# High parts of q and k stored once and loaded by two transfers, and chains of four pieces between the matrices

## The chip, the cores and the metric

The kernel runs on one core of a Trainium2 chip. The metric is the device time of one execution in microseconds; before the change its median is 2924.13 over three runs (2922.39 to 2925.51). All of the work is on five engines of that core (TensorE or PE, VectorE or DVE, ScalarE or ACT, GpSimd or POOL, and SyncE or SP, which only issues transfers here) and its 16 DMA engines.

## The reference

Two independent results stand side by side in one output of 2048 x 2048: multi-head attention with 32 heads of 32 columns, and a two-dimensional Fourier transform as matrix products.

```python
def _A_ref(x, wqkv, wo):                       # x: 2048 x 1024
    qkv = (x @ wqkv).reshape(B, S, 3, H, Dh) ...
    scores = jnp.einsum("bhqd,bhkd->bhqk", q, k) * scale
    p = _softmax(scores, axis=-1)
    o = jnp.einsum("bhqk,bhkd->bhqd", p, v)
    return o.transpose(...).reshape(B, S, D) @ wo

def _B_ref(x, dft_seq_re, dft_seq_im, dft_hid_re, dft_hid_im):
    a = jnp.einsum("bsd,ed->bse", x, dft_hid_re)
    b = jnp.einsum("bsd,ed->bse", x, dft_hid_im)
    return jnp.einsum("ts,bse->bte", dft_seq_re, a) - jnp.einsum("ts,bse->bte", dft_seq_im, b)
```

All inputs are float32.

## The kernel before

**Arithmetic.** The matrix products take operands rounded to fewer bits, so each operand is split into a high part (the rounded value) and a low part (the rest), and a product is made of three matmuls: high x high, low x high, high x low. The large products (q, k, v, the Fourier matrices, the output projection) are cut by a scheme with seven products in place of eight; its operands are sums and differences of blocks, called pieces here. A piece is loaded (`fetch`), added or subtracted on POOL or DVE, and split by `halves`: the high part by a cast (L501 on DVE, L499 on ACT), the low part by a subtraction (L504). `piece` makes stationary operands in the tile hl, `moving` makes moving operands in a slot (20 numbered buffers, taken through `take_slot`).

**Attention.** For a head h the scores are made twice. `scores(h)` makes them with rows as queries (L1853, tile psS: 32 steps of two matmuls, each followed by a maximum on DVE, L1859, and an exponential on ACT, L1862), which gives each row's maximum and sum. `transposed(h)` makes them again transposed (L1975, psT: 64 matmuls, each with an exponential, L1979) and multiplies the result with v (L1994). The high and low parts of q and k are stacked along the contraction: QS[h % 2] holds q in 96 rows (for each of the 32 components the high, the low and again the high part), KS[h % 2] holds k (high, high, low). So one matmul makes all three products. Rows 96 and 97 of QS take the maxima: zeros (z_d, L2016) for `scores`, then the negative maxima in two parts, which travel over DRAM (store m_d<-lt, L1900; load qs<-m_d, L1901) and open `transposed(h)`. The first four query blocks of `scores(h)` read a copy of the first 512 columns, QX, so that they can begin while QS still serves the head before last.

**q and k over DRAM.** The projections write q and k for four heads at a time: `store_qk(b, j, part, t)` stores a block of 128 rows x 512 columns to `qk_d[b][j]`, a tile [128, 3, 512]. The high part goes out twice in one transfer (L294, a broadcast source, 512 KB), the low part once (L292, 256 KB), so that the three rows of one component lie together. `load_qk` (L312) reads 32 components x 3 = 96 rows of 512 columns in one transfer of 192 KB, eight a head, as soon as the buffers of the head before last are free: one for each quarter of k, after every fourth round of `transposed`, and four for q at its end. `load_x` (L1839) loads QX in the same way.

**The order.** Nothing is ordered on the chip. When the kernel is built, the class `Plan` simulates all engines with costs per operation and emits the instructions of each in the order of this simulation. PE takes from four streams: the score matmuls (S), the transposed ones (T), the value products (V) and the fills, which are all other matmuls (L414). The other engines have heaps: the operations that are ready, lowest rank first, then the earlier ready time. A `Ring` passed as `order` makes the next operation wait until the one before it has begun (`o.soon`); its ready time is then that moment. On the chip each engine runs its list in order, so an instruction that waits holds the ones behind it.

**Around the change.** The Fourier part runs through `dense1`, first with seven outer products of the real matrix, then `between` (two of the second stage's products, p = 1 and 7, eight groups of 24 matmuls each, tile xk_d), then seven of the imaginary matrix. The imaginary half needs the same stationary pieces as the real half, so these are kept in DRAM (ha_d) and loaded again by `again` (L1585). Those that the real half doesn't make by itself are made aside: `aside_c` (L1262) makes chains of four (p = 5, 6, 3, 7; each sum starts from the one before, in three buffers of the tile c) and `aside` (L1303) makes single ones in a slot: two loads, a sum (L1332), for some a store of the sum (si_d, L1338), a cast (L1342), a difference (L1344), and a store of both parts (512 KB). `aside` also makes sums of the Fourier matrix ahead of time ("b" entries), which `load_r` later loads in place of two blocks and a sum. `between` calls `aside` three times in each of 12 groups, for 32 pieces.

## Time and profile before

| | |
|---|---|
| median of three runs | 2924.13 us |
| profiled execution | 2929.45 us, span 2927.7 us |
| granted TensorE clock | 0.999 of full speed |
| DMA traffic | 765.04 MB on the main queue, 79.4% of 16 engines' time |
| read from and written to HBM | 511.74 and 253.25 MB |

Two rows on DMA and one on the largest work of DVE help to place what follows:

```profile
q1 hardware_dynamic: 485452, 765.04, 79.4%
```

```profile
L1859 DVE TENSOR_REDUCE negm<-psS 128x1 f32<-128x1024 f32 x1024 | 1240.7, 1221 | 198.3 <-PE psS L1853 190.1
```

The second is a group of the page: line, engine, operation, tiles and shapes, count, then busy time in us and the mean of one in ns, then the time that the engine stood idle before such instructions and what ended it. A row of the issue list gives tiles, queue, operation, count and KB of one transfer. In the timeline the first number is the start in us from the span's start, the second how long it took. SP's rows are issues: the time to issue a transfer, not to carry it.

### The profile page before, as it was taken

How to read it: one execution, taken by the hardware profiler on the slowest of the kernel's cores; microseconds unless marked ns; L12 is line 12 of the kernel's file. 1: busy time of each engine (PE TensorE's matmuls, PEld its weight loads, DVE VectorE, ACT ScalarE, POOL GpSimd, SP SyncE). 2: the span in 40 equal slices, each digit the busy share in tenths (PEclk: the TensorE clock that was granted, in tenths of full speed). 3: DMA queues.
4: the chain of work that ended last, by engine and by line, in shares of the span. 5: the costliest groups of instructions: out<-in, count | busy, mean ns of one | idle time of the engine just before them, and what ended most of it. 6: DMA issues, size and time to landing. Idle time of an engine off the chain costs nothing.

```text
span 2927.7 us, 47039 instructions
## 1 busy us (share of the span) xinstructions
PE 2904.0 (99%) x14728; PEld 2107.2 (72%) x14728; DVE 2386.5 (82%) x3251; ACT 2373.3 (81%) x4509; POOL 1241.3 (42%) x975
## 2 busy tenths in 40 slices
PE   9999999999999999999999999999999999999999
PEld 8887776777667777777676677667667777777777
DVE  7679888788788887788888898888988788788745
ACT  5348898888888888988999898898889888888741
POOL 2325534142233433337655456666675352243200
PEclk9999999999999999999999999999999999999999
DMA  9989978697789988867899776887876665677558
GB/s 345 349 298 328 314 225 272 222 346 269 268 289 339 309 297 287 291 213 218 291 348 333 226 223 216 276 272 229 271 229 208 204 180 181 193 246 226 188 191 287
DMA packets 485844, 768.18 MB, mean 262 GB/s; under 512 B 120382, under 2 KB 153406, under 8 KB 485470
## 3 DMA queue, kind: packets, MB, share of 16 engines
q1 hardware_dynamic: 485452, 765.04, 79.4%
q8 instruction: 119, 1.95, 0.3%
q14 instruction: 129, 1.06, 0.1%
q10 hardware_dynamic: 144, 0.13, 0.0%
HBM read 511.74 MB, written 253.25 MB: 261 GB/s over the span
## 4 chain that ended last, share of the span: by engine, by line
PE 75%; DMA 4%; DVE 1%; ACT 1%; SPq 0%; issue 0%; POOL 0%; DVEq 0%; ACTq 0%; POOLq 0%
PE pd L414 34%; PE psT L1975 14%; PE pd L1994 13%; PE psS L1853 13%; PE psT L414 2%; ACT psS L1862 1%; DVE negm L1859 1%; DMA qs<-m_d 1%; DMA slot<-in_ct 0%; DMA g<-in_ct 0%; DMA hl<-ha_d 0%; ACT pt L1979 0%; DMA m_d<-lt 0%; DMA ha_d<-slot 0%; DMA g<-g_d 0%
## 5 line engine op out<-in xcount | busy, mean ns | idle before, releaser
L414 PE MATMUL pd<-slot,hl 128*128 128x512 f32 x5028 | 1446.7, 390 | 4.2 <-DMA hl<-ha_d 1.4
L1979 ACT ACTIVATE pt<-psT 128x512 f32<-128x512 f32 x2048 | 1191.5, 668 | 260.7 <-PE psT L1975 258.5
L1859 DVE TENSOR_REDUCE negm<-psS 128x1 f32<-128x1024 f32 x1024 | 1240.7, 1221 | 198.3 <-PE psS L1853 190.1
L1862 ACT ACTIVATE psS<-psS,negm 128x1024 f32<-128x1024 f32 x1024 | 1189.2, 1161 | 47.4 <-DVE negm L1859 44.5
L414 PEld LDWEIGHTS pd<-slot,hl 128*128 128x128 f32 x5028 | 943.6, 188 | 204.8 <-DVE negm L1859 2.7
L1975 PE MATMUL psT<-qs,ks 128*128 128x512 f32 x2048 | 802.4, 395 | 4.4 <-DMA qs<-m_d 3.2
L1975 PEld LDWEIGHTS psT<-qs,ks 128*128 128x128 f32 x2048 | 382.2, 188 | 160.0 <-issue 53.0
L1853 PE MATMUL psS<-ks,qs 128*128 128x512 f32 x1552 | 473.1, 391 | 4.2 <-ACT psS L1862 4.2
L1994 PE MATMUL pd<-pt,vt 128*32 128x512 f32 x4096 | 460.9, 596 | 1.2 <-DVE e L723 0.9
L1853 PEld LDWEIGHTS psS<-ks,qs 128*128 128x128 f32 x1552 | 289.5, 188 | 69.1 <-ACT psS L1862 11.0
L504 POOL TENSOR_TENSOR slot<-raw,slot 128x512 fp32r<-128x512 f32 x153 | 196.2, 1291 | 316.1 <-DVE slot L501 116.6
L1994 PEld LDWEIGHTS pd<-pt,vt 128*32 128x32 f32 x4096 | 123.4, 110 | 285.1 <-issue 268.3
L504 POOL TENSOR_TENSOR slot<-slot,slot 128x512 fp32r<-128x512 f32 x183 | 234.3, 1292 | 206.1 <-DVE slot L501 54.5
L1862 ACT ACTIVATION_READ_ACCUMULATOR psS<-psS,negm 128x1 f32 x1024 | 287.0, 280 | 0.0
L504 POOL TENSOR_TENSOR hl<-raw,hl 128x512 fp32r<-128x512 f32 x122 | 156.8, 1289 | 257.4 <-DVE hl L501 84.7
L479 POOL TENSOR_TENSOR raw<-raw,g 128x512 f32<-128x512 f32 x119 | 153.3, 1291 | 226.6 <-ACT pt L1979 31.3
L414 PE MATMUL pd<-slot,slot 128*128 128x512 f32 x780 | 210.6, 389 | 0.1
L414 PEld LDWEIGHTS pd<-slot,slot 128*128 128x128 f32 x780 | 146.4, 188 | 30.9 <-DVE e L723 0.4
L1853 PE MATMUL psS<-ks,qx 128*128 128x512 f32 x496 | 151.0, 394 | 3.3 <-ACT psS L1862 3.2
L479 DVE TENSOR_TENSOR raw<-raw,g 128x512 f32<-128x512 f32 x141 | 103.3, 738 | 23.6 <-DMA g<-in_ct 6.6
L1853 PEld LDWEIGHTS psS<-ks,qx 128*128 128x128 f32 x496 | 91.7, 188 | 34.6 <-issue 9.2
L479 POOL TENSOR_TENSOR slot<-slot,slot 128x512 f32<-128x512 f32 x79 | 102.1, 1302 | 27.5 <-DVE slot L479 11.3
(140 smaller groups left out, 2167.6 us busy)
## 6 DMA issues: line engine op xcount, KB each, us to landing
hl<-ha_d SPq DMA_DIRECT2D x134, 512.0 KB
slot<-in_ct SPq DMA_DIRECT2D x144, 256.0 KB
qk_d<-e SPq DMA_DIRECT2D x52, 512.0 KB
qs<-qk_d SPq DMA_DIRECT2D x128, 192.0 KB
ks<-qk_d SPq DMA_DIRECT2D x128, 192.0 KB
raw<-g_d SPq DMA_DIRECT2D x96, 256.0 KB
ha_d<-hl SPq DMA_DIRECT2D x42, 512.0 KB
raw<-in_ct SPq DMA_DIRECT2D x80, 256.0 KB
```

The lines of the kernel that those rows point to most:

```text
L414: nc.tensor.matmul(box["ps"], a[1]((a[0].hi, a[0].lo)[u]()), b[1]((b[0].hi, b[0].lo)[v]()), start=k == 0, stop=k == n - 1)
L479: (nc.gpsimd if e == "POOL" else nc.vector).tensor_tensor(out=dest(), in0=dest() if a is None else a.get(), in1=other["q"] if "q" in other ...
L504: (nc.gpsimd if e == "POOL" else nc.vector).tensor_tensor(out=lo(), in0=raw(), in1=f(hi()), op=ALU.subtract)
L1853: nc.tensor.matmul(p[:, i * NB : i * NB + NB], (QX[0] if own else QS[h % 2])[:, qt * P : qt * P + P], KS[h % 2][:, c * 1024 + i * NB : c * ...
L1859: nc.vector.tensor_reduce(out=ST["negm"][:, c, qt : qt + 1], in_=box["p"], axis=AX.X, op=ALU.max, negate=True)
L1862: nc.scalar.activation(box["p"], box["p"], AF.Exp, bias=ST["negm"][:, c, qt : qt + 1], accum_out=ST["sums"][:, c, qt : qt + 1])
L1975: nc.tensor.matmul(box["p"], KS[h % 2][:, t * P : t * P + P], QS[h % 2][:, j * NB : j * NB + NB], start=True, stop=True)
L1979: nc.scalar.activation(box["t"], box["p"], AF.Exp)
L1994: nc.tensor.matmul(po["p"][j * DH : j * DH + DH, :], VT[h][:, k, :], box["t"], start=(k == t0), stop=(k == t), tile_position=(0, j * DH),)
```

## The change

`qk_d` becomes two tiles per block of four heads, [128, 2, 2, 512]: component, part, half, column. Each part is stored once, 256 KB. `rows` puts the 96 rows together by two transfers, now with the 32 components of a part side by side: rows 0 to 63 from both parts in turn (q, x) or from the high part twice (k), and rows 64 to 95 from the part that is left. From head 2 on one pair of transfers covers two quarters (1024 columns: 256 and 128 KB), so a head has four pairs; heads 0 and 1 have eight pairs of half the size. For QX there are two transfers, 128 and 64 KB. The last pair for k is issued at the end of `transposed`, with both pairs for q. A pair is linked by a Ring, so the second waits until the first has begun.

In `between` the 32 single pieces are replaced by eight chains of four, in three sets of two slots each; each of the 12 groups advances each set by one step. `aside_c` takes the chain, the list and the slots as arguments for this. The sums si_d of these pieces are no longer stored and loaded, and a kept piece is stored by two transfers of 256 KB. Six sums of the Fourier matrix are made there too, and the projections make ten more of them ahead (steps 5 and 6 as well).

```diff
-    qk_d = [[dram.tile([P, 3, NB], F32, name=f"qk_d{b}_{j}") for j in range(4)] for b in range(16)]
+    qk_d = [[dram.tile([P, 2, 2, NB], F32, name=f"qk_d{b}_{j}") for j in range(2)] for b in range(16)]
...
-        d = qk_d[b][j]
-        if part:
-            nc.sync.dma_start(d[:, 2 if b % 2 else 1, :], f(t))
+        nc.sync.dma_start(qk_d[b][j // 2][:, part, j % 2], f(t))
+
+    def rows(dst, src, which, again):
+
+        if again:
+            nc.sync.dma_start(dst[2 * DH : 3 * DH], src[:, which])
+        elif which:
+            nc.sync.dma_start(dst[0 : 2 * DH], src[:, 0].rearrange("d (o c) -> o d c", o=1).broadcast_to([2, DH, src.shape[2]]))
         else:
-            nc.sync.dma_start(d[:, 0:2, :] if b % 2 else d[:, 0:3:2, :], f(t).rearrange("p (o n) -> p o n", o=1).broadcast_to([P, 2, NB]))
+            nc.sync.dma_start(dst[0 : 2 * DH], src.rearrange("d i c -> i d c"))
...
-        nc.sync.dma_start(dst[0 : 3 * DH, j * NB : j * NB + NB], qk_d[2 * g + which][j][r0 * DH : r0 * DH + DH].rearrange("d i c -> (d i) c"))
+        src = qk_d[2 * g + which][j // 2][r0 * DH : r0 * DH + DH]
+        rows(dst[:, j * NB : (j + n) * NB], src.rearrange("d i j c -> d i (j c)") if n == 2 else src[:, :, j % 2], which, again)
...
                 if n:
                     aside_c()
-                elif x > 6:
+                else:
                     aside((12, 13, 14))
...
-    def aside_c():
+    def aside_c(chain=chain, todo=todo_c, places=None):
...
-        left = [(pp, p, i, None) for pp in ORDER for p in (5, 6, 3, 7) for i in range(2) if (pp, p, i) not in kept_a]
-        rest = [t for t in todo_a if t[1] == "b"][:0]
...
+        sets = [({}, [], (19, 18)), ({}, [], (17, 16)), ({}, [], (15, 14))]
+        left = [(pp, i) for pp in ORDER for i in range(2) if (pp, 5, i) not in kept_a]
+        for n, (pp, i) in enumerate(left):
+            sets[n % 3][1].extend((pp, p, i) for p in (5, 6, 3, 7))
+        todo_a[:] = [t for t in todo_a if t[1] == "b"][:6]
...
-                    for _ in range(count):
-                        aside((19, 18, 17, 16, 15, 14))
+                    for one in sets:
+                        aside_c(*one)
+                    aside((13, 12))
...
-        got[h, which, j] = op("SP", ISSUE, lambda: load_qk(h, which, j), [*qk_st[2 * g + which][j], *after], [], -2, 192)
+        n = 2 if h > 1 and True else 1
+        both = Ring(1)
+        for again in range(2):
+            o = op("SP", ISSUE, lambda again=again: load_qk(h, which, j, again, n), [*(o for k in range(n) for o in qk_st[2 * g + which][j + k]), *after], [], -2, n * (128 - 64 * again), both)
+        for k in range(n):
+            got[h, which, j + k] = o
...
-                nc.sync.dma_start(f(QX[0])[0 : 3 * DH], qk_d[2 * g][0][r0 * DH : r0 * DH + DH].rearrange("d i c -> (d i) c"))
...
+                rows(f(QX[0]), qk_d[2 * g][0][r0 * DH : r0 * DH + DH, :, 0], 0, again)
...
-            if t % 4 == 3 and h + 2 < H:
-                load_qk_op(h + 2, 1, t // 4, [Tops[h][-1], Sops[h][-1]])
+            if t % 8 == 7 and h + 2 < H:
+                load_qk_op(h + 2, 1, t // 8 * 2, [Tops[h][-1], Sops[h][-1]])
         if h + 2 < H:
-            for j in range(4):
+            for j in (0, 2):
                 load_qk_op(h + 2, 0, j, [Tops[h][-1], Sops[h][-1]])
```

More of the change, by code (lines that the diff above doesn't have):

```diff
@@ L304, with load_qk @@
     nc.gpsimd.memset(rec, 1.0)
-    def load_qk(h, which, j):
+    def load_qk(h, which, j, again, n=1):
         g, r0 = divmod(h, 4)
@@ L1260, with get @@
     chain = {}
-    def aside_c():
-        if not todo_c:
+    def aside_c(chain=chain, todo=todo_c, places=None):
+        if not todo:
             return
-        pp, p, i = todo_c.pop(0)
+        pp, p, i = todo.pop(0)
         rank = seq() + LATER
-        if p == 5:
+        ring = CR if p == 5 and places is None else None
+        if p == 5 and places:
+            chain["n"] = []
+            for k in places:
+                old, users = take_slot(k)
+                box = {}
+                def get(half, k=k, box=box):
+                    if "t" not in box:
+                        box["t"] = slot(k, [P, 2, NB])
+                    return f(box["t"])[:, half]
+                chain["n"] += [[lambda half=half, get=get: get(half), users, old] for half in range(2)]
+            chain["n"] = [chain["n"][2], *chain["n"][:2]]
+        elif p == 5:
             chain["n"] = []
@@ L1291, in aside_c @@
         high = op("DVE", CAST, lambda e: nc.scalar.activation(t().bitcast(F32R), s(), AF.Copy) if e == "ACT" else nc.vector.tensor_copy(t().bitcast(F32R), s()), [made], [us, ut], 10 + rank, other=("ACT", ACAST, 25 + rank), two=True)
-        low = op("POOL", SUB, lambda e: (nc.gpsimd if e == "POOL" else nc.vector).tensor_tensor(out=l().bitcast(F32R), in0=s(), in1=t(), op=ALU.subtract), [high, *wl], [us, ut, ul], rank, 0, CR if p == 5 else None, other=("DVE", ADD, 25 + rank), two=True)
+        low = op("POOL", SUB, lambda e: (nc.gpsimd if e == "POOL" else nc.vector).tensor_tensor(out=l().bitcast(F32R), in0=s(), in1=t(), op=ALU.subtract), [high, *wl], [us, ut, ul], rank, 0, ring, other=("DVE", ADD, 25 + rank), two=True)
         kept_a[pp, p, i] = [op("SP", ISSUE, lambda n=n, r=r: nc.sync.dma_start(ha_d[pp][p][i][:, n * NB : n * NB + NB], r()), [m], [u], rank, 256) for n, (r, m, u) in enumerate(((t, high, ut), (l, low, ul)))]
```

13 lines of the change are left out of this document (6 added, 7 removed).

## The prediction

> **What bounds the kernel now.** I read the page's busy shares and chain first, then what PE loses to waiting, then the DMA share by stage, and last the queue of transfers where one head ends and the next begins.
>
> ```profile
> span 2927.7 us, 47039 instructions
> PE 2904.0 (99%) x14728; PEld 2107.2 (72%) x14728; DVE 2386.5 (82%) x3251; ACT 2373.3 (81%) x4509; POOL 1241.3 (42%) x975
> PE 75%; DMA 4%; DVE 1%; ACT 1%; SPq 0%; issue 0%; POOL 0%; DVEq 0%; ACTq 0%; POOLq 0%
> DMA packets 485844, 768.18 MB, mean 262 GB/s; under 512 B 120382, under 2 KB 153406, under 8 KB 485470
> ```
>
> ```profile
> L414 PE MATMUL pd<-slot,hl 128*128 128x512 f32 x5028 | 1446.7, 390 | 4.2 <-DMA hl<-ha_d 1.4 <-DVE negm L1859 1.3 <-POOL hl L504 0.8
> L1994 PE MATMUL pd<-pt,vt 128*32 128x512 f32 x4096 | 460.9, 596 | 1.2 <-DVE e L723 0.9 <-DVE c L671 0.2
> ```
>
> ```profile
> 2841.29 10.88 PE psT L414 x48
> ```
>
> ```profile
> 1216.66 5.29 PE pd L1994 x48
> ```
>
> PE advances by 10.88/48 = 0.227 us for a full matmul and 5.29/48 = 0.110 for one of the narrow value matmuls. So (14728 - 4096) x 0.227 + 4096 x 0.110 = 2864 us of the span is matmuls at their own pace. All waiting together is 64 us: **this is the most that any change outside PE can gain**, and the projections' matmuls (L414), which the new chains feed, lost only 4.2. PE's order is fixed when the kernel is built, so a PE instruction whose data is late holds all that stand behind it; with 64 us of slack in 2928, lateness is paid in full.
>
> The DMA engines by stage (columns: us, busy time of each engine, granted clock, DMA share, GB/s):
>
> ```profile
> 73.00:146.00 73.00, 72.53 (x321) 59.68 (x320) 47.84 (x74) 23.00 (x39) 24.56 (x19) 1.00 1.00 349
> 572.00:1215.00 643.00, 639.61 (x3306) 455.52 (x3305) 529.28 (x707) 561.32 (x1074) 228.98 (x179) 1.00 0.89 301
> 1215.00:1374.00 159.00, 159.00 (x828) 114.17 (x827) 133.99 (x182) 140.08 (x269) 83.42 (x66) 1.00 0.73 223
> 1374.00:1616.00 242.00, 239.29 (x1231) 167.85 (x1230) 213.19 (x293) 219.07 (x419) 143.00 (x113) 1.00 0.94 317
> 1616.00:2267.00 651.00, 644.65 (x3329) 460.30 (x3329) 568.25 (x767) 569.86 (x1095) 395.70 (x312) 1.00 0.75 239
> 2267.00:2811.00 544.00, 543.58 (x2835) 388.94 (x2835) 431.01 (x598) 458.07 (x876) 176.22 (x138) 1.00 0.64 201
> 1425.00:1635.00 210.00, 205.58 (x1063) 142.55 (x1062) 183.67 (x252) 187.60 (x359) 113.30 (x89) 1.00 0.96 327
> ```
>
> Sixteen engines at share 1.00 move 349 GB/s, **21.8 GB/s each**. The shares are means over sixteen: a transfer that fewer engines carry loads those few.
>
> **How many engines carry a transfer.** From the issue list, whose 101 rows (first and last below) count 3019 transfers:
>
> ```profile
> hl<-ha_d SPq DMA_DIRECT2D x134, 512.0 KB
> ...
> qs<-qk_d SPq DMA_DIRECT2D x128, 192.0 KB
> ks<-qk_d SPq DMA_DIRECT2D x128, 192.0 KB
> ...
> vt<-v_d SPq DMA_DIRECT2D x128, 64.0 KB
> ...
> qx<-qk_d SPq DMA_DIRECT2D x31, 192.0 KB
> ...
> m_d<-lt SPq DMA_DIRECT2D x32, 16.0 KB
> qs<-m_d SPq DMA_DIRECT2D x32, 16.0 KB
> r_d<-ll SPq DMA_DIRECT2D x32, 16.0 KB
> qs<-z_d SPq DMA_DIRECT2D x30, 16.0 KB
> ...
> z_d<-qs SPq DMA_DIRECT2D x1, 16.0 KB
> ```
>
> The data pieces under 512 B are the 128-byte rows of vt (128 transfers of 512 rows) and of m_d and r_d (64 of 128): 73,728. The page counts 120,382 such packets, so 46,654 are left, about one per transfer and engine. 3019 x 16 would be 48,304: 1,650 are missing. The transfers whose outermost dimension is small are the 63 with two rows (qs<-m_d, qs<-z_d, z_d) and the 64 that go out as "g i p" with g = 4 (m_d, r_d). If the first ran on 2 engines and the second on 4, 63 x 14 + 64 x 12 = 882 + 768 = 1,650 are missing, which is the count exactly. For m_d one side is 4 blocks and the other 128 partitions: the smaller one decides.
>
> The Trainium skill states this as a rule: in "DMA: Bandwidth & Descriptors", section "Why a DMA increments its semaphore by 16 and not by 1", the engine count is the largest k up to 16 that divides the outermost dimension on both sides, the lowest-numbered k engines take it, and section "Rules for kernel authors" warns that a leading zero-stride broadcast of c copies confines a DMA to c engines. The count above agrees. That page's 27 GiB/s per engine would make the burst worked out below 13.6 us instead of 18.0.
>
> **The loads of q and k: the term that decides.** `rows` replaces one transfer of 96 rows by two. The first of each writes 64 rows from a source "i d c" (q, x) or "o d c" (k, a broadcast): outermost dimension 2. So it runs on 2 engines like qs<-m_d. The second has 32 rows and spreads. No row shows which two carry a transfer; I take the same two each time (if they changed, the three firsts below would run side by side in 6 us, which the lower bound covers). Per head from 2 on: four first transfers of 256 KB and one of 128 KB (x), 589,824 B on each of the two engines, 27.1 us at 21.8; the second ones add 1.7; the nine old loads took 9 x 192 KB/16 = 110,592 B, 5.1 us. **Net +23.7 us of two engines per head.**
>
> Where it hurts is the head boundary. SP's queue there (start, us, instruction):
>
> ```profile
> 1214.39 0.55 SPq L1900 DMA_DIRECT2D m_d<-lt  x1
> 1215.03 0.41 SPq L312 DMA_DIRECT2D ks<-qk_d  x1
> 1215.50 1.82 SPq L312 DMA_DIRECT2D qs<-qk_d  x4
> 1217.82 0.23 SPq L1901 DMA_DIRECT2D qs<-m_d  x1
> 1218.09 0.25 SPq L2016 DMA_DIRECT2D qs<-z_d  x1
> ```
>
> ```profile
> 1294.66 0.43 SPq L312 DMA_DIRECT2D ks<-qk_d  x1
> 1295.14 1.82 SPq L312 DMA_DIRECT2D qs<-qk_d  x4
> 1298.09 0.23 SPq L1901 DMA_DIRECT2D qs<-m_d  x1
> ```
>
> and PE's at the same place:
>
> ```profile
> 1211.73 0.62 PE L1853 MATMUL psS<-ks,qx 128*128 128x512 f32 x2
> ...
> 1213.77 0.62 PE L1853 MATMUL psS<-ks,qx 128*128 128x512 f32 x2
> ...
> 1216.04 0.61 PE L1853 MATMUL psS<-ks,qx 128*128 128x512 f32 x2
> 1216.59 5.36 PE L1994 MATMUL pd<-pt,vt 128*32 128x512 f32 x48
> 1221.87 1.21 PE L1853 MATMUL psS<-ks,qx 128*128 128x512 f32 x4
> 1222.92 0.62 PE L1975 MATMUL psT<-qs,ks 128*128 128x512 f32 x2
> ```
>
> As one head's last transposed matmul ends, the last of k and all of q for the head after next are issued; 79.6 us later again. The first four score steps (two matmuls each) use the first half of k, the fifth, at 1222.4, the second half; then qs<-m_d opens the transposed head at 1222.92. Before, the five loads put 5 x 192 KB/16 = 61,440 B on an engine, 2.8 us, and PE hardly waits.
>
> After, three first transfers (k's second half, q's two halves) put 3 x 128 KB = 393,216 B on each of the two engines: 18.0 us. k's second transfer becomes ready only when its first has begun, with a later ready time at the same rank, so the planner's heap issues both q firsts ahead of it; it spreads over all engines and so stands behind them on those two, and qs<-m_d, itself a two-engine transfer, mostly behind them too. The floor from issue to landing is about 3 us (m_d<-lt at 1214.39, its follower qs<-m_d released at 1217.82). So k is whole at 1215.03 + 18.0 + 0.7 + 3 = 1236.7, 14.3 after the fifth score step was due. Behind that step on PE stand T's matmuls, the fills and, through them, DVE and ACT: nothing covers it. SP, in order too, stands at reused landing slots meanwhile.
>
> Upper bound 14.3 us per boundary. Lower bound: k's second transfer goes ahead of the q ones (1215.03 + 6.0 + 0.7 + 3 = 1224.7, 2.3 late), and half of the boundaries have qs<-m_d behind the burst (13 late) and half ahead of it: about 7, or 6 with the two engines a tenth faster. The 21.8 was measured with sixteen engines pulling at once, two alone can only be faster, so I take 11, on the upper side because both gates point there. There are 30 boundaries (heads 2 to 31): **+330** (180 to 430).
>
> Two engines' load in between: a head of the stage from 572 needs 0.89 x 79.6 + 23.7 = 94.5 us of them, against 90.6 that it then lasts: about 4 x 8 heads, of which the halved stores give some back: **+20**. Elsewhere (0.94 x 79.6 + 23.7 - 8 for the chains = 90.5; 83 and less) the stretched head holds it.
>
> **The stores of q and k.** The high part is written once: 64 x 256 KB = 16.8 MB less, 48 us of sixteen engines, spread over the projection stages, where PE did not wait for it: 0 by itself.
>
> **The chains between the matrices.** Eight chains of four. One before: 8 loads, 2 sums stored, 4 kept pieces of 512 KB, 4.7 MB in 14 transfers; after: 6 loads and 8 stores of 256 KB, 3.7 MB in 14. 8.4 MB less in a stage with share 0.96 where PE lost 210 - 205.6 = 4.4 us: **-4 at best**. A step is a load, a sum, a cast and a difference, in series:
>
> ```profile
> L1332 POOL TENSOR_TENSOR slot<-slot 128x512 f32<-128x512 f32 x38 | 49.9, 1314 | 85.2 <-DMA slot<-in_ct 35.4 <-DMA slot<-so_d 11.7 <-DVE hl L504 9.0
> ```
>
> about 3.4 + 1.3 + 0.6 + 1.3 = 7 us. The longest of the three queues has 3 chains, 12 steps, 84 us, under the 12 groups of this stage of 210 us with 16. POOL, 42% busy, hides it; without that cover the kept pieces would be late by one step, 7 us.
>
> **Sixteen more sums ahead** (10 in the projection, 6 between): their adds are moved, not added; they add 16 loads and 10 stores of 256 KB, 6.8 MB, in stages where the stores saved more. **Issues**: 16 (heads 0 and 1) and 31 (x) more, 47 x 0.42 = 20 us of SP over the run: 0. Taken with the chains: **-5** (bounds -9 and +7).
>
> **Sum.** The profiled execution took 2929.45 with the span 2927.7; 2929.45 + 330 + 20 - 5 = 3274. It stood 5.3 over the median of 2924.13, so I forecast **3270**; with the bounds of the boundary 3115 to 3370, and a further 30 if the load of the two engines is not absorbed.
>
> **Rivals.** *The boundary is covered and only the two engines' load counts.* The planner would have to place the fifth step and T's start late. For it: other loads are issued well ahead. Against: both gates are within 8 us of the issue now. Heads then last what two engines need: 14.9 x 8.1 heads from 572, 2.2 x 2, (18.9 - 8) x 3, 3.8 x 8.2, together 189, less 20 for the stores: about 3090.
>
> *The transfers spread over sixteen engines after all*, because their sides are regrouped into 64 rows before they go out. From that point the loads cost 0.2 us more issue each and nothing else; the kernel gains the 5 of the chains: 2929.45 - 5 - 5.3 = **2919**. Against it stands m_d, whose 4 against 128 was not regrouped.
>
> *The queue cascades*: at 14.3 per boundary and with SP so late after each that the dense stages add 5 per head over 11 heads: 2929 + 430 + 55 + 20 - 5 - 5 = 3424.
>
> **How the numbers follow.** Forecast 0.77, covered boundary 0.09, spread transfers 0.08, cascade 0.06. The range 3080 to 3400 holds the forecast's bounds and the covered case. A measurement tells 0.2% (6 us) from no change: the spread case gives faster 0.06 and same 0.02; all others are slower, 0.92.
>
> **What would show it.** Right: packets under 512 B fall far below sixteen per transfer (each first transfer leaves 14 fewer: 4 x 30 + 16 + 31 = 167 of them, 2338); PE's idle time before L1853 and L1975 grows by some 300 us with ks<-qk_d, qs<-qk_d or qs<-m_d as releasers; the mean DMA share falls in the middle stages while heads last about 90 us. Wrong: heads stay near 80 us, or PE's lost time lies at L414, which would put the cause in the chains, or the DMA share stays as it is with no such waits.

## The result, and the profile after

| | before | after |
|---|---|---|
| median, four runs each | 2923.26 us (2920.92 to 2925.51) | 3509.33 us (3501.55 to 3514.67) |
| ratio, 95% interval | | 1.2003 (1.1977 to 1.2029) |
| profiled execution | 2929.45 us, span 2927.7 | 3511.76 us, span 3510.0 |
| granted TensorE clock | 0.999 | 0.926 |

The change makes the kernel 20% slower, against 3270 us forecast and 3080 to 3400 as the range. Lines have moved: L1853, L1975, L414 and L1994 of before are L1879, L2001, L418 and L2020 here; the first transfer of `rows` is L297 for k and L299 for q and QX, the second is L295 for all.

The page of after: span, PE's busy share, the packets, and the chain that ended last, by engine.

```profile
span 3510.0 us, 47212 instructions
PE 3001.6 (86%) x14728; PEld 2162.9 (62%) x14728; DVE 2388.5 (68%) x3244; ACT 2384.1 (68%) x4505; POOL 1252.1 (36%) x986
DMA packets 468290, 749.82 MB, mean 214 GB/s; under 512 B 119212, under 2 KB 152236, under 8 KB 467916
PE 62%; DMA 25%; DVE 5%; SPq 4%; issue 2%; ACT 2%; POOL 0%; DVEq 0%; POOLq 0%; ACTq 0%
```

DVE, ACT and POOL do the same work as before, within 12 us each. PE's matmuls are as many as before; its busy time grew by 98 us, and the span by 582, so the rest is waiting. Transfers hold 25% of the chain, where they held 4%.

The same page's groups for the matmuls (busy us and mean ns of one, then idle before and what ended it):

```profile
L2001 PE MATMUL psT<-qs,ks 128*128 128x512 f32 x2048 | 825.4, 407 | 194.9 <-DMA qs<-m_d 185.9
L1879 PE MATMUL psS<-ks,qx 128*128 128x512 f32 x496 | 175.7, 448 | 248.8 <-DMA ks<-qk_d 194.3
L418 PE MATMUL pd<-slot,hl 128*128 128x512 f32 x5064 | 1490.6, 397 | 4.8 <-DVE ot L2033 4.2
```

The waiting stands before the two matmuls that open a boundary: the score steps that read the copy QX, and the transposed head's first. The projections' and Fourier matmuls (L418) lose 4.8 us, against 4.2 before: the loss does not stand at the matmuls that the chains feed. The list of what PE waited for in the trace of after (us in total, times, longest):

```profile
PE psS L1879 <- DMA ks<-qk_d: 205.3, 19, 17.4
PE psT L2001 <- DMA qs<-m_d: 185.9, 20, 16.7
PE psS L1879 <- ACT psS L1888: 41.3, 25, 20.2
PE psS L1879 <- DMA u_d<-slot: 14.2, 1, 14.2
```

One boundary in the timeline of after, SP's issues first (start, us, instruction), then PE's:

```profile
2945.66 0.52 SPq L297 DMA_DIRECT2D ks<-qk_d  x1
2946.23 0.56 SPq L299 DMA_DIRECT2D qs<-qk_d  x1
2946.88 0.51 SPq L1927 DMA_DIRECT2D qs<-m_d  x1
2947.45 0.50 SPq L299 DMA_DIRECT2D qs<-qk_d  x1
2948.00 0.47 SPq L2042 DMA_DIRECT2D qs<-z_d  x1
2948.51 2.70 SPq L295 DMA_DIRECT2D ks<-qk_d  x1
```

```profile
2946.29 0.61 PE L1879 MATMUL psS<-ks,qx 128*128 128x512 f32 x2
2946.74 0.61 PE L418 MATMUL pd<-slot,slot 128*128 128x512 f32 x2
2947.29 5.36 PE L2020 MATMUL pd<-pt,vt 128*32 128x512 f32 x48
2960.20 1.22 PE L2001 MATMUL psT<-qs,ks 128*128 128x512 f32 x2 [7.56 <-DMA qs<-m_d]
2961.22 1.05 PE L1879 MATMUL psS<-ks,qx 128*128 128x512 f32 x2
2967.04 1.19 PE L1879 MATMUL psS<-ks,qx 128*128 128x512 f32 x2 [4.76 <-issue]
```

k's first transfer goes out at 2945.66, its second only at 2948.51, after both q firsts. The row m_d is issued at 2946.88 between the q firsts and opens PE's gate at 2960.20. The steps after it stop again until 2967.04; the profile names no releaser there, but what they read is k's second half, whose second transfer was issued last.

The trace's semaphore events show when these transfers land. k's first is there at 2954.8, q's firsts at 2960.0 and 2965.9, m_d's row at 2960.2: one after another and not side by side, so the same two engines carry them. Of the sixteen shares of k's second transfer fourteen land by 2953.3; the last two land at 2965.7 and 2967.0, and PE starts at 2967.04. At all 30 boundaries k's second transfer is issued behind both q firsts.

**The clock.** Stretches of after around one such wait, which lasts from 487.4 to 502.0 (columns: us, busy time and count of PE, weight loads, DVE, ACT, POOL, then the granted clock, DMA share and GB/s):

```profile
480.00:487.40 7.40, 7.40 (x58) 2.88 (x57) 6.04 (x9) 5.02 (x11) 2.16 (x2) 1.00 0.27 76
487.40:492.10 4.70, 0.36 (x2) 0.00 (x0) 0.69 (x2) 0.78 (x2) 0.00 (x0) 1.00 0.13 51
492.10:502.00 9.90, 0.01 (x1) 0.04 (x1) 0.00 (x0) 0.00 (x0) 0.00 (x0) 0.50 0.37 124
502.00:505.70 3.70, 3.70 (x9) 2.92 (x10) 2.36 (x2) 1.20 (x3) 2.06 (x2) 0.50 0.99 295
505.70:560.00 54.30, 52.70 (x273) 38.09 (x272) 43.85 (x56) 48.67 (x93) 25.31 (x21) 1.00 0.68 220
```

The granted clock falls to 0.50 at 4.7 us into the wait and comes back 3.7 us after PE has begun to work again; in those 3.7 us PE makes nine matmuls, where at full clock there would be 3.7/0.227 = 16. The wait is paid, and then some more.

The stretch of heads that answers to the stage from 572 before:

```profile
579.40:1275.10 695.70, 583.24 (x2882) 410.26 (x2875) 461.93 (x611) 492.19 (x935) 190.53 (x149) 0.92 0.68 225
```

The DMA share fell from 0.89 to 0.68 while the kernel waits for transfers. Most of the fall is the same traffic over a longer head (the last transposed matmul of head 2 ends at 576.2, that of head 9 at 1275.1, 99.8 us a head: 0.89 x 79.6/99.8 = 0.71). What it says is that the sixteen engines together are not what is short; how busy the two are, no row shows.

**Where the 582 us of span went.** For each run I summed the gaps between the starts of successive matmuls on PE, less the normal 0.227 us (0.110 after a value matmul). Gaps over 1.2 us are waits; those on score steps 5 to 10 of heads 2 to 31 and the first two transposed matmuls stand at a boundary. What is left, gaps under 1.2 us, is PE's pace, in which the clock shows. After: boundary waits 421, other waits 85, pace 128. Before: 4, 5 and 44. The differences, **417 at the boundaries, 80 elsewhere and 84 in pace**, add to 581. As a check on the last: the granted clock was at half for 190 us in which PE wasn't waiting (5 before), which costs (190 - 5)/2 = 93.

### The profile page after: what moved, and what is told of

Read it like the earlier page. It is cut to its first block, busy times and chain, and to the rows that moved or that the text cites. A ratio compares the mean times of both kernels' runs of the same rounds, so it can differ in the third digit from the quotient of the medians.

```text
span 3510.0 us, 47212 instructions
## 1 busy us (share of the span) xinstructions
PE 3001.6 (86%) x14728; PEld 2162.9 (62%) x14728; DVE 2388.5 (68%) x3244; ACT 2384.1 (68%) x4505; POOL 1252.1 (36%) x986
## 2 busy tenths in 40 slices
DMA packets 468290, 749.82 MB, mean 214 GB/s; under 512 B 119212, under 2 KB 152236, under 8 KB 467916
## 3 DMA queue, kind: packets, MB, share of 16 engines
HBM read 511.74 MB, written 234.90 MB: 213 GB/s over the span
## 4 chain that ended last, share of the span: by engine, by line
PE 62%; DMA 25%; DVE 5%; SPq 4%; issue 2%; ACT 2%; POOL 0%; DVEq 0%; POOLq 0%; ACTq 0%
PE pd L418 29%; PE psT L2001 11%; PE psS L1879 11%; DMA ks<-qk_d 9%; PE pd L2020 7%; DMA qs<-m_d 5%; PE psT L418 3%; SPq L2042 2%; DVE negm L1885 2%; DMA m_d<-lt 1%; DMA qk_d<-e 1%; SPq L299 1%; ACT psS L1888 1%; DMA ha_d<-c 1%; DMA qs<-qk_d 1%
## 5 line engine op out<-in xcount | busy, mean ns | idle before, releaser
L418 PE MATMUL pd<-slot,hl 128*128 128x512 f32 x5064 | 1490.6, 397 | 4.8 <-DVE ot L2033 4.2
L1888 ACT ACTIVATE psS<-psS,negm 128x1024 f32<-128x1024 f32 x1024 | 1175.9, 1148 | 154.1 <-DVE negm L1885 151.8
L418 PEld LDWEIGHTS pd<-slot,hl 128*128 128x128 f32 x5064 | 977.7, 193 | 215.8 <-DVE ot L2033 5.0
L2001 PE MATMUL psT<-qs,ks 128*128 128x512 f32 x2048 | 825.4, 407 | 194.9 <-DMA qs<-m_d 185.9
L2001 PEld LDWEIGHTS psT<-qs,ks 128*128 128x128 f32 x2048 | 394.7, 195 | 363.4 <-DMA qs<-m_d 200.4
L1879 PE MATMUL psS<-ks,qs 128*128 128x512 f32 x1552 | 479.0, 394 | 33.8 <-ACT psS L1888 21.1
L2020 PE MATMUL pd<-pt,vt 128*32 128x512 f32 x4096 | 465.8, 601 | 15.5 <-DVE e L675 5.2
L1879 PE MATMUL psS<-ks,qx 128*128 128x512 f32 x496 | 175.7, 448 | 248.8 <-DMA ks<-qk_d 194.3
L1879 PEld LDWEIGHTS psS<-ks,qs 128*128 128x128 f32 x1552 | 289.8, 189 | 105.8 <-ACT psS L1888 33.4
L483 POOL TENSOR_TENSOR raw<-raw,g 128x512 f32<-128x512 f32 x145 | 186.8, 1296 | 441.0 <-DVE hl L508 35.9
L2020 PEld LDWEIGHTS pd<-pt,vt 128*32 128x32 f32 x4096 | 124.3, 111 | 303.4 <-issue 268.0
L1879 PEld LDWEIGHTS psS<-ks,qx 128*128 128x128 f32 x496 | 103.6, 216 | 287.1 <-issue 244.4
L1888 ACT ACTIVATION_READ_ACCUMULATOR psS<-psS,negm 128x1 f32 x1024 | 272.5, 266 | 0.0
L418 PE MATMUL pd<-slot,slot 128*128 128x512 f32 x780 | 215.5, 393 | 1.7 <-DVE ot L2033 1.7
L418 PEld LDWEIGHTS pd<-slot,slot 128*128 128x128 f32 x780 | 148.0, 190 | 33.3 <-DVE ot L2033 2.5
L483 DVE TENSOR_TENSOR raw<-raw,g 128x512 f32<-128x512 f32 x115 | 85.5, 750 | 51.6 <-DMA g<-g_d 7.6
```

The source lines that it names most:

```text
L418: nc.tensor.matmul(box["ps"], a[1]((a[0].hi, a[0].lo)[u]()), b[1]((b[0].hi, b[0].lo)[v]()), start=k == 0, stop=k == n - 1)
L483: (nc.gpsimd if e == "POOL" else nc.vector).tensor_tensor(out=dest(), in0=dest() if a is None else a.get(), in1=other["q"] if "q" in other ...
L1879: nc.tensor.matmul(p[:, i * NB : i * NB + NB], (QX[0] if own else QS[h % 2])[:, qt * P : qt * P + P], KS[h % 2][:, c * 1024 + i * NB : c * ...
L1888: nc.scalar.activation(box["p"], box["p"], AF.Exp, bias=ST["negm"][:, c, qt : qt + 1], accum_out=ST["sums"][:, c, qt : qt + 1])
L2001: nc.tensor.matmul(box["p"], KS[h % 2][:, t * P : t * P + P], QS[h % 2][:, j * NB : j * NB + NB], start=True, stop=True)
L2020: nc.tensor.matmul(po["p"][j * DH : j * DH + DH, :], VT[h][:, k, :], box["t"], start=(k == t0), stop=(k == t), tile_position=(0, j * DH),)
```

## Experiments

Twelve kernels. Ratios are against runs of the kernel before on the same chip (medians 2919 to 2923).

| run | median us | ratio, 95% interval | clock |
|---|---|---|---|
| e1, spread over sixteen engines | 2956.59 | 1.0109 (1.0091 to 1.0127) | 0.997 |
| e2, two-engine loads without the chains | 3519.80 | 1.2039 (1.2010 to 1.2067) | 0.928 |
| e3, chains and sums without the loads | 2925.46 | 1.0010 (1.0000 to 1.0020) | 0.999 |
| e4, three spread transfers | 2934.79 | 1.0042 (1.0026 to 1.0058) | 1.000 |
| e5, two engines for k alone | 3270.74 | 1.1199 (1.1166 to 1.1231) | 0.957 |
| e6, two engines for q and QX alone | 3290.23 | 1.1265 (1.1230 to 1.1301) | 0.950 |
| e7, k's second transfer ahead | 3429.02 | 1.1740 (1.1706 to 1.1775) | 0.946 |
| e8, spread, burst put at mid-head | 3218.33 | 1.1019 (1.0987 to 1.1051) | 0.962 |
| e9, spread and k's second ahead | 2945.79 | 1.0075 (1.0062 to 1.0088) | 0.998 |
| e10, as e9 without chains and sums | 2937.03 | 1.0043 (1.0029 to 1.0056) | 1.000 |
| e11, chains alone | 2927.30 | 1.0014 (1.0005 to 1.0023) | 0.998 |
| e12, k's first read as q's | 3485.68 | 1.1931 (1.1911 to 1.1951) | 0.927 |

### e1: the same transfers, spread

```diff
-            nc.sync.dma_start(dst[0 : 2 * DH], src[:, 0].rearrange("d (o c) -> o d c", o=1).broadcast_to([2, DH, src.shape[2]]))
+            nc.sync.dma_start(dst[0 : 2 * DH], src[:, 0].rearrange("d (o c) -> d o c", o=1).broadcast_to([DH, 2, src.shape[2]]))
...
-            nc.sync.dma_start(dst[0 : 2 * DH], src.rearrange("d i c -> i d c"))
+            nc.sync.dma_start(dst[0 : 2 * DH], src.rearrange("d i c -> (d i) c"))
```

> The changed kernel, with the 64 rows of each first transfer in another order: component by component (the two rows of a component side by side) in place of part by part. Bytes, number of transfers, stores and chains stay; the outermost dimension becomes 32 or 64 instead of 2. Theory (the first transfers run on two engines and hold up the head boundary): the waits before the fifth score step and before the first transposed matmul go, the granted clock returns to 0.99 or more, heads last about 80 us again, and the time is 2915 to 2930. Rival 1 (two transfers per load, or their issue, are what costs, whatever engines carry them): about 3500, unchanged. Rival 2 (the chains between the matrices or the sums made ahead cost): 3000 or more, with PE waiting at the projections' matmuls.

2956.59 us. The number of transfers, their bytes and their issues are those of the changed kernel; only the order of the 64 rows differs, so that the outermost dimension is 32 or 64 in place of 2. Of the 586 us, 553 are gone. The page's packets and PE's waits in e1:

```profile
DMA packets 470628, 749.83 MB, mean 254 GB/s; under 512 B 121550, under 2 KB 154574, under 8 KB 470254
```

```profile
PE psS L1879 <- ACT psS L1888: 9.2, 13, 2.8
PE psT L2001 <- DMA qs<-m_d: 7.0, 7, 2.3
PE psS L1879 <- DMA ks<-qk_d: 5.1, 3, 2.9
```

121550 - 119212 = 2338 small packets more than after, which is 167 first transfers x 14 engines: **each first transfer of the change ran on two engines**. The semaphore events of after say it without this count: for each of the 167 firsts there are three, one within 0.6 us of the issue's end and two as data lands, and for each second transfer sixteen. The 33 us that remain over before were not expected. The waits in the trace are 24 us against 9, with ks<-qk_d and qs<-m_d among the releasers: the same gates, a little late. e9 and e10 look at them.

### e2 and e3: the two halves of the change

e2 is the changed kernel with the single pieces of before between the matrices and none of the extra sums; e3 is the kernel before with the chains, the six sums and the ten sums, and its old path of q and k. The core of e3's diff (e2 is its reverse, against the changed kernel):

```diff
-        left = [(pp, p, i, None) for pp in ORDER for p in (5, 6, 3, 7) for i in range(2) if (pp, p, i) not in kept_a]
...
+        sets = [({}, [], (19, 18)), ({}, [], (17, 16)), ({}, [], (15, 14))]
...
-                    for _ in range(count):
-                        aside((19, 18, 17, 16, 15, 14))
+                    for one in sets:
+                        aside_c(*one)
+                    aside((13, 12))
```

> The changed stores and loads of q and k alone; the pieces between the matrices and the sums made ahead as before the change. Theory: all of the loss is here, 3490 to 3530. Rival (the chains have a part in it): clearly less than 3490, by what the chains cost.

> The chains and the sums made ahead alone; q and k stored and loaded as before the change. Theory: within 10 us of the kernel before, more likely 3 to 8 below it (2915 to 2925), with si_d gone and the DMA share of the stage between the matrices lower. Rival: the chains cost, 2940 or more, with waits at the projections' matmuls.

e2 took 3519.80 us, so the loads make the whole loss. e3 took 2925.46: the chains and sums give no gain. Both signs of a few us were possible by the forecast's bounds; the -5 it took was not there.

### e4: three spread transfers

As the change, but each part goes by a transfer of its own, 32 rows in natural order:

```diff
+        part = ((0, 1, 0), (0, 0, 1))[which][again]
+        nc.sync.dma_start(dst[again * DH : again * DH + DH], src[:, part])
...
+        for again in range(3):
+            o = op("SP", ISSUE, lambda again=again: load_qk(h, which, j, again, n), [*(o for k in range(n) for o in qk_st[2 * g + which][j + k]), *after], [], -2, n * 64, both)
```

> The changed kernel with three transfers of 32 rows per load in place of one of 64 and one of 32: the rows stand in the same order as in the changed kernel, part by part, but no transfer has an outermost dimension of 2. Theory: 2915 to 2940, a few us over the kernel with two spread transfers at most, for the issues. Rival 1 (the number of transfers costs): more than 3509, since there are half as many again. Rival 3 (the order of the rows itself costs, for instance in the destination's partitions): about 3500.

2934.79 us, ratio 1.0042. Half as many issues again as in the change cost little. So neither the layout with each part stored once nor several transfers to one buffer is the trouble. It is also 22 us faster than e1, on the same chip and with one transfer more per load (waits over 1.2 us: 11 us against 24). The two runs differ in the order of the rows too; what makes the 22 us was not tried.

### e5, e6 and e7: which of the loads, and in which order

e5 leaves only k's firsts on two engines, e6 only q's and QX's; the others go as two transfers of 32 rows. e7 is the changed kernel with k's second transfer ahead of q's firsts.

```diff
-            nc.sync.dma_start(dst[0 : 2 * DH], src.rearrange("d i c -> i d c"))
+            for i in range(2):
+                nc.sync.dma_start(dst[i * DH : i * DH + DH], src[:, i])
```

```diff
-            nc.sync.dma_start(dst[0 : 2 * DH], src[:, 0].rearrange("d (o c) -> o d c", o=1).broadcast_to([2, DH, src.shape[2]]))
+            for i in range(2):
+                nc.sync.dma_start(dst[i * DH : i * DH + DH], src[:, 0])
```

```diff
-            o = op("SP", ISSUE, lambda again=again: load_qk(h, which, j, again, n), [*(o for k in range(n) for o in qk_st[2 * g + which][j + k]), *after], [], -2, n * (128 - 64 * again), both)
+            o = op("SP", ISSUE, lambda again=again: load_qk(h, which, j, again, n), [*(o for k in range(n) for o in qk_st[2 * g + which][j + k]), *after], [], -2 - 0.5 * which * again, n * (128 - 64 * again), both)
```

> The changed kernel with only k's first transfers left on two engines; those of q and x are issued as two transfers of 32 rows, which spread. At a boundary one two-engine transfer of 256 KB is left instead of three. In the changed kernel three of them (3 x 5.3 us between landings) cost a wait of 14.5 us, so the boundary covers about 1.4 us. Theory (the length of the burst at the boundary less its cover): waits of 5.3 - 1.4 = 4 us, hardly any time at half clock, 2940 + 30 x 5.5 = 3100 (3020 to 3160). Rival (the bytes on the two engines count, 12.1 of 27.1 us a head): 2945 + 0.45 x 565 = 3200, with the DMA engines as the limit all along the head.

> The changed kernel with only the first transfers of q and x left on two engines; k's are issued as two transfers of 32 rows, which spread. Two two-engine transfers of 256 KB are left at a boundary, and k's last rows still stand behind them. Theory: waits of 10.6 - 1.4 = 9 us and about 4 us lost at half clock after each, 2940 + 30 x 13.4 + 20 = 3360 (3200 to 3420). Rival (bytes): 2945 + 0.55 x 565 = 3256. Rival (k's own slow transfer is what the score steps wait for): below 3050.

> The changed kernel with k's second transfer given a better rank, so that it is issued right behind k's first one and ahead of q's. All two-engine transfers stay. Theory (two gates behind one burst): the fifth score step waits about 4 us instead of 13, but where qs<-m_d is issued behind the burst the first transposed matmul still waits for all of it, so part of the loss goes: 3300 to 3450, with the waits for ks<-qk_d much smaller and those for qs<-m_d larger. Rival (the order on the queue does not matter, the load does): 3490 to 3530.

| run | boundary waits, us per head | other waits, us | half clock outside waits, us | median us |
|---|---|---|---|---|
| after | 14.0 | 85 | 190 | 3509 |
| e5 (k) | 6.7 | 66 | 183 | 3271 |
| e6 (q, QX) | 9.5 | 22 | 152 | 3290 |
| e7 (k's second ahead) | 9.9 | 102 | 202 | 3429 |

e5 missed its theory and its rival, both too low. The waits of PE in e5 (its lines stand one further):

```profile
PE psT L2002 <- DMA qs<-m_d: 105.8, 21, 9.1
PE psS L1880 <- DMA ks<-qk_d: 90.3, 15, 10.9
```

One 256 KB transfer on two engines holds up a boundary by 6.7 us. Its own service is 8.0 us in the median (how that is taken stands at e12), and m_d's row, also on two engines, is behind it. The half clock, which costs 183/2 = 91 us here, was in neither expectation. e6 lies within its range: two such transfers, 9.5 us per head, where the theory said 9. (Its rival by bytes, 3256, lies in the same range, so the time alone doesn't part them; e5's rival by bytes, 3200, was 71 too low.) In e7 the order is mended, and PE's waits change place:

```profile
PE psT L2001 <- DMA qs<-m_d: 166.8, 20, 14.6
PE psS L1879 <- ACT psS L1888: 100.2, 42, 18.2
PE psS L1879 <- DMA ks<-qk_d: 55.6, 18, 6.1
```

The wait for k falls from 205.3 to 55.6, the wait for m_d's row stays near its 185.9 (larger had been expected), and 59 us more than after's 41.3 stand at ACT. Order gives back 80 us of 586; **the number of engines gives back 553 (e1)**.

### e8: the same burst where PE has other work

e1 with three two-engine copies of 256 KB added early in each of 28 heads; they copy parts of q and k within DRAM to a place that nothing reads.

```diff
+            if t == 3 and 1 < h < H - 2:
+                for i in range(3):
+                    more = dram.tile([2, DH, 2 * NB], F32, name=f"more{h}_{i}")
+                    op("SP", ISSUE, lambda i=i, more=more: nc.sync.dma_start(more, qk_d[2 * (h // 4) + i // 2][i % 2][h % 4 * DH : h % 4 * DH + DH].rearrange("d i j c -> i d (j c)")), [Tops[h][-1]], [], -2, 256)
```

> The kernel with spread transfers (2957 us) and, in 28 heads, three extra copies of 256 KB from DRAM to DRAM with an outermost dimension of 2 on both sides, issued together after a quarter of the transposed matmuls, in the middle of the head; nothing waits for them. So the two engines carry the same burst of some 16 us a head as in the changed kernel, away from the boundary. Theory (the place is what costs: at the boundary PE waits for what stands behind the burst, in the middle its loads were issued ahead): 2960 to 3120. Rival (two engines loaded by 24 us a head hold up everything, wherever): over 3300.

3218.33 us, between the two. The boundary waits are gone (0.6 us per head), but the same burst of three costs (3218.33 - 2956.59) / 28 = 9.4 us per head away from the boundary, clock included; at the boundary its waits alone were 14.0. The copies are also 768 KB of new traffic a head, and that the two engines cost and not these bytes rests on the landings below. One place in the timeline of e8, for DVE, ACT and PE in turn:

```profile
1213.74 0.69 DVE L483 TENSOR_TENSOR raw<-raw,g 128x512 f32<-128x512 f32 x1 [11.18 <-DMA g<-in_ct]
```

```profile
1214.52 0.63 ACT L503 ACTIVATE slot<-raw 128x512 fp32r<-128x512 f32 x1 [11.86 <-DVE raw L483]
```

```profile
1215.69 0.80 PE L2001 MATMUL psT<-qs,ks 128*128 128x512 f32 x1 [8.59 <-ACT pt L2005]
```

The trace has the semaphore events of these transfers. The three copies, issued at 1192.35 to 1193.72, land at 1201.9, 1206.8 and 1211.8, some 5 us apart, each in two shares 0.4 to 0.5 us apart. The load g<-in_ct, 256 KB over all sixteen, was issued at 1199.73. Its shares land like this:

```
1202.6 1202.6 1202.9 1203.0 1203.0 1203.0 1203.0 1203.0 1203.1 1203.1 1203.6 1203.7 1203.8 1203.9
1213.3 1213.7
```

Fourteen engines are done by 1203.9; **two bring the rest 9.8 us later**, after the last copy has landed and 0.4 us apart like its shares. No row names an engine; that these are the two which carry the copies is read from this pattern. DVE, in order, stands at it for 11.18 us, ACT stands behind DVE's sum, and PE, whose transposed scores need an exponential from ACT, stands behind both. So the boundary makes a burst dearer, but this place in mid-head did not make it free.

### e9, e10 and e11: what stays when the engines are right

e9 is e1 with e7's edit. e10 is e9 with the single pieces of before and no extra sums. e11 is the kernel before with the chains alone, without e3's sixteen sums:

```diff
-        todo_a[:] = [t for t in todo_a if t[1] == "b"][:6]
+        todo_a[:] = [t for t in todo_a if t[1] == "b"][:0]
...
-                else:
+                elif x > 6:
                     aside((12, 13, 14))
```

> Rows put together component by component (64 rows outermost, so all engines carry each load) as in the run that took 2956.6, and in addition the second transfer of k is given a rank half a step ahead, so that it is issued before the q firsts. Theory: the 33 us that the spread version still lost against before are SP's order at the boundary (the fifth score step waits 1 to 3 us for the second transfer of k, which is issued behind three others). Then these waits go: 2920 to 2945 us, granted clock above 0.998. Rival: they come from one more landing per load wherever it is issued, or from the later q and m_d rows: 2950 to 2962, as without the edit.

> As the run before, but the chains between the matrices and the extra sums ahead are as they were before the change: only the stores of the high parts and the loads (spread, the second of k ahead) are changed. Theory: the chains neither gain nor cost more than 5 us, so it lies within 6 us of the run before, 2918 to 2945. Rival: chains and loads disturb each other, then it is over 10 us faster or slower than the run before.

> The path of q and k as before the change; only the chains of four between the matrices, without any of the 16 sums of the Fourier matrix made ahead. Both together measured 1.001 of before (1.000 to 1.002), where -5 us had been forecast. Theory: the sums ahead cost what the chains gain, so the chains alone take 2916 to 2922. Rival: PE had nothing to win there, 2922 to 2928.

PE's waits in e9:

```profile
PE psS L1879 <- ACT psS L1888: 12.1, 13, 4.7
PE psT L2001 <- DMA qs<-m_d: 5.5, 6, 1.5
...
PE psS L1879 <- DMA ks<-qk_d: 1.2, 1, 1.2
```

The waits for k went (5.1 to 1.2), and the time fell from 2956.59 to 2945.79, which is 0.8 us outside the theory's range: by the ratios SP's order was a third of e1's loss. The trace shows only a part of that: the profiled executions differ by 4.6 us, the waits over 1.2 us by 4. The single pieces in e10 bring it to 2937.03, 8.8 us below e9, more than the theory's 6 and less than the rival's 10; the intervals of the two ratios do not meet, so with these loads the chains and sums cost something. By themselves they cost 3 to 4 us by the ratios of e3 and e11, and since e11 is no faster than e3, the sums ahead are not what ate the gain: the rival holds. The +14 that e10 keeps over before is **open**: its waits over 1.2 us sum to 12 against 9, and its profiled span is 4.1 over before's, so the trace shows only a part. e4, with the chains but another order of the rows, keeps as much (1.0042 against 1.0043). No version here is faster than before.

### e12: are two engines on the same rows slower?

In the changed kernel k's first transfer, which reads the high part twice, takes longer than q's of equal size. I took the service of such a transfer as the time from when the transfer before it landed (or from 1.3 us after its issue, whichever is later) to its own landing: 7.1 us for k's, 5.2 for q's, in the median.

```diff
-            nc.sync.dma_start(dst[0 : 2 * DH], src[:, 0].rearrange("d (o c) -> o d c", o=1).broadcast_to([2, DH, src.shape[2]]))
+            nc.sync.dma_start(dst[0 : 2 * DH], src.rearrange("d i c -> i d c"))
```

> The changed kernel, with one difference: the first transfer of k reads the high and the low part in turn, as q's does, instead of the high part twice (so k's rows 32 to 63 hold the low part and the scores differ from the reference's). Engines, sizes, issue order and everything else stay. In the changed kernel k's first transfer of 256 KB is served in 7.1 us (median), q's in 5.2. Theory: the two engines read the same rows of DRAM at the same time and are slower for it; then k's first is served in about 5.2 here, the wait per boundary falls from 14.0 by about 1.9 to 12.1 us, and the run is about 30 x 1.9 = 57 us faster than the changed kernel: 3430 to 3475. Rival: k's is slower because it is the first of the burst and has other transfers' remainders before it on the two engines; then its service stays near 7 us and the run at 3500 to 3520.

3485.68 us: neither range. k's first is still served in 6.9 us and the boundary waits are 13.7 per head. The theory of the shared rows falls as the main cause; reading them once each is worth 24 us, of 57 expected. What makes k's first longer is mostly something else, and stays open; whether it is the remainders of the transfers before it was not tried. A part is the count itself: it takes off 1.3 us for the way from issue to landing, while the quickest 16 KB row of m_d takes 1.8 us (in the trace of before; 2.0 in after's). A transfer that opens a burst bears the difference, those behind it don't.

PE's two main waits in e12 show the same picture as after's:

```profile
PE psS L1879 <- DMA ks<-qk_d: 187.5, 19, 17.1
PE psT L2001 <- DMA qs<-m_d: 178.8, 19, 15.1
```

## Why the prediction was right, and where it was wrong

The mechanism came as forecast, but the sum did not: 3509 us lies above the range of 3080 to 3400, because one term was too small (the wait per boundary), one far too small (the waits elsewhere) and one missing (the clock).

**What bounds the kernel: right.** "Lateness is paid in full" holds: 497 us of added waits on PE, 84 of pace, 582 of span.

**Two engines carry each first transfer: right**, to the packet (2338, e1 against after). That they are the same two each time, which had to be assumed, the landings at the boundary above show. The Trainium skill's rule in "DMA: Bandwidth & Descriptors", section "Rules for kernel authors", that a leading broadcast of c copies confines a transfer to at most c engines, is what this trace shows, and q's "i d c" without a broadcast goes the same way. So the rival of spread transfers, 2919, falls as a forecast; as a kernel (e1 with its order) it isn't a gain either.

**The burst of 18.0 us: right.** Two q firsts of 5.2 us and k's of 7.1 make 17.5; the 13.6 that the prediction set beside it was too short.

**The wait per boundary, "so I take 11": this step failed first.** Measured 14.0, 421 - 4 = 417 in all, at the upper bound of 14.3. Three things were to make it lower. k's second transfer was not ahead of q's firsts (2948.51 behind 2947.45, and so at every boundary); the planner's order that I had read in the code was the real one, and I gave half its weight to the other. Two engines alone are indeed faster per transfer, 128 KB in 5.2 us or 25 GB/s, but k's 7.1 took this back. And m_d's row, ahead of the burst at half of the boundaries in the lower bound, saves nothing by being early: the fifth score step and the transposed head's first matmul stand next to each other on PE, and the one that is late holds the other. In the trace of after, from start to start on PE, head 18's fifth step waits 14.6 us and the transposed matmul beside it 0.5; at head 4 it is 0.4 and 14.6; at head 14 the two share it, 7.1 and 8.5. Even with k's order mended (e7) the wait is 9.9, not 6 or 7.

**The clock: missing from the sum.** Thirty waits of 11 us were forecast, and nothing was charged for PE's half clock after each. It is 84 us by the pace, 93 by the clock's own record. I could have known: the Trainium skill, "TensorE: Matmul & The Clock Gate", section "HAM oscillation — how this bites in real kernels", says that a wait longer than about 3.4 us puts the next stretch of matmuls at half clock. The windows above agree (half clock from 4.7 us into the wait); the trace of before, with the clock at 0.999, could not show it.

**Load in between, +20: too small.** Waits elsewhere grew by 80. Of after's 85, 20.3 is one wait at the start of head 1 (the 20.2 of the row `ACT psS L1888: 41.3, 25, 20.2`), 19 are shorter waits elsewhere in heads 0 and 1, and the rest are waits of 1 to 5 us in mid-head. Heads 0 and 1 had been priced as 16 more issues, at 0. The 20.3 us come from SP:

```profile
249.55 2.58 SPq L299 DMA_DIRECT2D qx<-qk_d  x1
...
266.82 0.45 SPq L467 DMA_DIRECT2D raw<-in_wqk  x1
```

```profile
271.71 0.43 DVE L505 CAST hl<-raw 128x512 fp32r<-128x512 f32 x1 [20.59 <-DMA raw<-in_wqk]
```

Behind head 1's eight half-size firsts single issues take SP some 2.6 us, where the median is 0.4. So raw<-in_wqk goes out only at 266.82; DVE stands 20.59 us for it, ACT behind DVE, and PE behind ACT until 274.63, though head 1's QX was there at 261.6. Over the run 60 issues took longer than 1.5 us, 202 us together, against 9 and 16 us before. For mid-head, e8 shows how a burst reaches PE there: DVE and ACT are in order, and a late load of other work stops them for PE too. The forecast held that the stretched head absorbs it.

**Stores 0, chains -5.** Written bytes fell from 253.25 to 234.90 MB; no run changes the stores alone, and none shows a gain that could be theirs. The chains and sums measure some 3 us on the other side alone (e3, whose interval reaches 1.000), the chains without the sums 4 (e11): the sign was wrong, the size within the bounds given.

**The sum.** In place of 330 + 20 - 5 = 345 the span shows 417 + 80 + 84 = 581. A third of the miss is the clock, a third the wait per boundary, a quarter the load elsewhere. The rival of the cascade came nearest in time (3424) with another mechanism: it priced the boundary rightly at 14.3 and then put the rest on SP's lateness. SP is late indeed (4% of the chain, 0% before, and the wait of head 1), but that rival leaves out the clock too, 84 us, and how much of the waits in mid-head is SP's was not separated. The rival of the covered boundary falls: 417 of the 582 stand there.

**What was to show it.** Packets and releasers came as said, and the DMA share fell (mostly because the heads grew longer). PE idled 391 us for the two releasers named, where "some 300" was said; heads last 97 us (the last transposed matmul of head 1 ends at 479.5, that of head 31 at 3394.0: 2914.5/30), where 90 was said.

## What to carry to other kernels

Count engines before bytes: give every transfer an outermost dimension that many engines can share, on both sides, above all when a rearranged or broadcast source puts a 2 in front (the same rows in another order gave back 553 of 586 us). A queue of narrow transfers delays the wide ones behind it, here at the head boundary (after) and in mid-head (e8), and can delay the issues themselves. And when a stall on PE is priced, add the half clock after it: here a sixth again of the waits.

## What the runs showed of the hardware

- In after the granted clock fell to 0.50 at 1 to 6 us into each wait of more than 10 us and came back 3 to 6 us past its end (4.7 and 3.7 in the windows shown). No wait of 3 us or more was without it, either inside or some 2 us behind at most. Every stretch at half clock, save the one that the end of the run cuts off, is a multiple of 3.4 us long (3.4, 6.8, 13.7, 17.1, 20.5 or 23.9). Over the run the time at half clock outside waits was 190 us, some 6 per boundary.
- Two late engines of sixteen make a wide transfer late: of g<-in_ct in e8 fourteen shares landed within 4.2 us of the issue, the last two after 14.
- Sixteen engines pulling together moved 21.8 GB/s each before; the two that carried a first transfer of q moved 128 KB each in 5.2 us, 25 GB/s.
- Behind a backlog on two engines SP's issues themselves took long: 60 of over 1.5 us in after (202 us together), 9 before (16 us).
